# Attention feeding a mixture of experts: the order in which GpSimd issues value and weight loads

## The chip, the cores and the metric

The kernel runs on one NeuronCore of a Trainium2 chip. The metric is the device time of one execution in microseconds. The time before the change is 408.86 us, the median of 3 runs (408.62 to 410.64). The profile is of one execution of 408.99 us; its span, from the first instruction to the last, is 407.1 us.

## What is computed

Two layers, one after the other. The first is causal attention with two kinds of heads: three "retrieval" heads see every earlier key, five "streaming" heads see 4 sink keys and a window of 64. The second is a mixture of four experts in which every token goes through every expert.

```python
# attention: batch 4, heads 8, sequence 768, head size 64
scores = scale * np.matmul(q, k.transpose(0, 1, 3, 2))
mask = np.where(retr, full_causal_mask, stream_mask)   # stream: causal & (sink | window)
a = softmax(np.where(mask, scores, -1e9))
x = np.matmul(a, v)            # -> 3072 tokens x 512
# experts: N 3072, D 512, E 4, F 1024
p = domain_probs / (domain_probs.sum(-1, keepdims=True) + 1e-09)
for e in range(E):
    h = np.maximum(x @ w1[e], 0.0)
    out += p[:, e:e + 1] * (h @ w2[e])
```

## The kernel before

**Tiles and stages.** The 3072 tokens are cut into 8 groups of 384 (`CH`): 4 batches times 2 chunks. Group g first needs attention for its chunk (`attention`, L473), which leaves 384 token columns in `xT`, and then the experts (`moe_group`, L824). For each expert the first layer multiplies w1 with `xT` (L840, 32 matmuls of 384 columns), ScalarE applies the relu into `hs` (L853), the second layer multiplies `hs` with w2 (L861, 24 matmuls of 512 columns), and VectorE adds the scaled result into `acc` (L873, L877). Inputs are 32-bit in device memory, matrices are kept in 16-bit.

**What is interleaved.** Attention of group 0 runs alone at the start, on the head of the timeline. From then on attention of group g+1 is woven into the experts of group g: the loop at L897 draws from a generator of attention steps according to an estimate of work spent. All engines follow the order of the program (`manual_schedule`, L93); nothing is reordered by a planner.

**Weights.** All of w1 and w2 stay in on-chip memory for the whole kernel (`w1sb`, `w2sb`). `load_w1(e, 0, F)` (L296) issues two loads of 512 KB in 16-bit, one for each half of the partitions; `load_w2(e)` (L304) issues one of 1024 KB. Every weight is loaded once, during the experts of group 0, and the first use of expert e in group 0 waits for it.

**Keys, queries and values of batch 0.** Chunk 0: `k` and `q` come in 32-bit through the queues of SyncE and ScalarE (L355, L368). Chunk 1: `k` and `q` are one load each on GpSimd's queue, `load_triples` (L209, issue at L211), transposed on TensorE at L488. The values of both chunks are loaded by head with `load_v(b, c, heads)` (L264): a retrieval head (0, 2, 6) goes into `vR` (L268), a streaming head (1, 3, 4, 5, 7) into `vS` (L274), 48 KB each for batch 0. TensorE multiplies `vR` at L634 and `vS` at L698. In attention of chunk 0 the last value products are those of heads 6, 5 and 7, in this order, with filler matmuls (`warm_up`, L385) between them. In attention of chunk 1 the heads follow in the order 0, 2, 1, 3, 6, 5, 7, 4.

**GpSimd's queue.** All loads that change the number type go through GpSimd, which issues them in program order. Each load signals one of eight completion semaphores, taken in turn; before a load is issued GpSimd waits until the load eight places ahead, which used the same semaphore, has landed. Between the loads GpSimd fills padding and ones (`zero`, L327; `one_values`, L334; both through L325) and makes masks (L394 to L442). The order around the change is written out by hand at L445 to L463. After it come the fills of `kRr` and `kSr`, `mask_w`, and the loads for later groups (`load_k` L218, `load_q` L205, `load_v`), issued as far as the semaphores and buffers allow.

The loads of L445 to L463, in order: values of chunk 0 for heads 2, 1, 3, 4, 5, 6, 7 (head 0 was issued earlier, at L377); w1 of expert 0; fills; w2 of expert 0; k and q of chunk 1; w1 of expert 1; values of chunk 1 for heads 0 to 7; w2 of expert 1; w1 and w2 of experts 2 and 3.

Of the kernel before, what the change touches and what calls it, by code (L numbers as in the profile page):

```python
# [17 lines left out]
def kernel(  # L18
# [35 lines left out]
    B, H, S, D = q.shape  # L54
    E, DM, F = moe_w1.shape
# [93 lines left out]
    def half(u):  # L149
        return slice(u * D, (u + 1) * D)  # L150
# [5 lines left out]
    def own_v(h):  # L156
        return half(PLACE[h][1])
# [10 lines left out]
    def v_tiles(b, c, h):  # L168

        if RETR[h]:  # L170
            return vR[b % 2][:, 3 * c : 3 * c + 3, RH.index(h), :]
        if b:
            return windows(vSf, c)[:, :, SH.index(h), :]
        return vS[:, c, :, SH.index(h), :]
# [10 lines left out]
    def rows_of(x, b, h, c):  # L185
        return x[b, h, c * CH : (c + 1) * CH, :].rearrange("(j p) d -> p j d", p=P)

    def tiles_of(x, b, h, c):
        return x[b, h, c * CH : (c + 1) * CH, :].rearrange("(t r) d -> r t d", r=TK)

    def windows_of(x, b, h, c):

        assert b > 0
        first = ((b * H + h) * S + c * CH - WO) * D
        return bass.AP(x.tensor, x.offset + first, [[D, P], [WQ * D, WT], [1, D]])
# [68 lines left out]
    def load_v(b, c, heads):  # L264
        for h in heads:
            t = v_tiles(b, c, h)
            if RETR[h]:
                gp.dma_start(out=t[:, :, 0:D], in_=rows_of(v, b, h, c))  # L268
            elif b:
                gp.dma_start(  # L270
                    out=t[:, :, own_v(h)], in_=windows_of(v, b, h, c)
                )
            else:
                gp.dma_start(  # L274
                    out=t[R0:P, :, own_v(h)],
                    in_=tiles_of(v, b, h, c),
                )
# [18 lines left out]
    def load_w1(e, f0, f1):  # L296
        x = moe_w1[e].rearrange("(u c d) f -> u d c f", u=2, c=DMP)
        for u in range(2):
            gp.dma_start(  # L299
                out=w1sb[half(u), e * DMP : (e + 1) * DMP, f0:f1],  # L300
                in_=x[u, :, :, f0:f1],
            )

    def load_w2(e):  # L304
        gp.dma_start(
            out=w2sb[:, e * FTP : (e + 1) * FTP, :],
            in_=moe_w2[e].rearrange("(fo fi) d -> fi fo d", fi=P),
        )
# [6 lines left out]
    def fill(eng, ap, value):  # L315
        ap = ap.bitcast(FP32)
        if eng is nc.scalar:
            src = ones[0 : ap.shape[0], :]
            if len(ap.shape) == 3:
                src = src.rearrange("p (a b) -> p a b", a=1)  # L320
            elif len(ap.shape) == 4:
                src = src.rearrange("p (a b c) -> p a b c", a=1, b=1)
            eng.copy(out=ap, in_=src.to_broadcast(list(ap.shape)))
        else:
            eng.memset(ap, value)  # L325

    def zero(eng, t):  # L327
        fill(eng, t.rearrange("p a b x -> p (a b x)"), 0.0)
# [5 lines left out]
    def one_values(eng, c):  # L334

        one_values_r(eng, 0, c)
        x = vS[:, c, :, :, :].rearrange("p t s x -> p s t x")
        fill(eng, x[0:R0, :, :, :].rearrange("p s t x -> p (s t x)"), ONES)
        fill(eng, x[:, 0:2, :, D:P], ONES)
        fill(eng, x[:, 2:5, :, 0:D], ONES)  # L340
# [63 lines left out]
    def mask_s(x, n, keep, drop):  # L404

        gp.memset(x, keep)
        gp.affine_select(
            out=x, in_=x, compare_op=ALU.is_ge, fill=drop,
            base=R0, pattern=[[0, n], [1, TQ]], channel_multiplier=-1,
        )  # L410
        gp.affine_select(  # L411
            out=x, in_=x, compare_op=ALU.is_ge, fill=drop,
            base=NW - 1 - R0, pattern=[[0, n], [-1, TQ]], channel_multiplier=1,
        )
        gp.memset(x[0:R0, :, :], drop)
        gp.memset(x[0:NS, :, 0:TK], keep)
        gp.affine_select(
            out=x[0:NS, 0, 0:TK], in_=x[0:NS, 0, 0:TK], compare_op=ALU.is_ge,
            fill=drop, base=-NW, pattern=[[1, TK]], channel_multiplier=-1,
        )  # L420
# [23 lines left out]

    mask_c(bC, 0.0, -60000.0)  # L445
    mask_s(bS[:, 0:2, :], 2, 0.0, -60000.0)
    load_v(0, 0, [2, 1, 3, 4, 5, 6, 7])
    load_w1(0, 0, F)
    zero(gp, kR[0][:, 1, :, :, :])
    zero(gp, kS[:, 1, :, :, :].rearrange("p t s x -> p s t x"))  # L450
    one_values(gp, 1)
    load_w2(0)
    k16 = att.tile([P, H, 3, D], FP16, name="k16", bufs=1)
    load_triples(k, k16, 0, 1)
    qt16 = att.tile([P, H, 3, D], FP16, name="q16", bufs=2)
    load_triples(q, qt16, 0, 1)
    load_w1(1, 0, F)
    load_v(0, 1, range(H))
    load_w2(1)
    for e in range(2, E):  # L460
        load_w1(e, 0, F)
        load_w2(e)
    mSf = mS.rearrange("p t x -> p (t x)")  # L463
    bSf = bS.rearrange("p t x -> p (t x)")
    mWf = mW.rearrange("p t x -> p (t x)")
# [505 lines left out]
```

The softmax here doesn't subtract the row's maximum and nothing guards it: scores larger than these inputs give would overflow.

## Time and profile before

| engine | busy, us | share of the span |
|---|---|---|
| TensorE, matmuls | 393.4 | 97% |
| TensorE, weight loads (beside the matmuls) | 222.4 | 55% |
| ScalarE | 218.7 | 54% |
| VectorE | 156.0 | 38% |
| GpSimd | 142.8 | 35% |

The granted TensorE clock has a mean of 0.987 over the span. GpSimd's own queue moved 20.98 MB, counted as stored, in the whole span.

The groups of the page that bear on the change (operation, count, busy time, mean of one, idle time before it):

```profile
L840 PE MATMUL pA<-xT,w1sb 128*128 128x384 f16 x1024 | 188.3, 329 | 3.3 <-DMA w1sb<-in_moe_w_dram 3.1
L861 PE MATMUL pO<-w2sb,hs 128*128 128x512 f16 x768 | 182.4, 381 | 2.8 <-DMA w2sb<-in_moe_w_dram 2.8
L268 POOL DMA_DIRECT2D vR<-in_v_dram x24 | 19.3, 805 | 1.7 <-DMA w1sb<-in_moe_w_dram 1.6
```

And its list of loads (count, size of one, median time from issue to landing):

```profile
w1sb<-in_moe_w_dram POOLq DMA_DIRECT2D x8, 512.0 KB, 14.7
w2sb<-in_moe_w_dram POOLq DMA_DIRECT2D x4, 1024.0 KB, 14.8
```

Busy time of TensorE is the duration of its matmuls as the profile models them; a matmul at half the granted clock counts as busy for longer. The last column of a group is idle time of that engine just before such an instruction, with the releaser that ended most of it. A time from issue to landing includes the time that a load spends in the queue behind earlier ones.

### The profile page before, as it was taken

The page shows a single profiled execution, that of the slowest core. Times are in us where ns is not written, and L with a number is a line of the kernel's source. Part 1 is how long each engine was busy: PE and PEld are TensorE (multiplying, and loading weights), DVE is VectorE, ACT ScalarE, POOL GpSimd, SP SyncE. Part 2 cuts the span into 40 slices and gives each one's busy share as a digit, 9 for nine tenths or more (in the row PEclk, how much of TensorE's full clock was granted, in tenths as well). Part 3 has the DMA queues.
Part 4 walks back from the last instruction along what each step waited for, and adds up shares of the span by engine and source line. Part 5 has one row for each costly group of instructions (what it writes and reads, how often), then busy time and mean ns, then how long its engine had stood idle before and what let it go on. Part 6 is the DMA issues. An engine that isn't in the chain of part 4 may idle for free.

```text
span 407.1 us, 7111 instructions
## 1 busy us (share of the span) xinstructions
PE 393.4 (97%) x2821; PEld 222.4 (55%) x2821; DVE 156.0 (38%) x343; ACT 218.7 (54%) x468; POOL 142.8 (35%) x179
## 2 busy tenths in 40 slices
PE   7896799999999999999999999999999999999996
PEld 4753455555555555555555555555555555655552
DVE  7736065423443223434443223434443223432222
ACT  4751447734575456854464555854564555753331
POOL 8934922924954911950009600870000000000000
PEclk9997889999999999999999999999999999999999
DMA  9999999999998989990389929991391100010001
GB/s 169 143 182 143 183 205 185 99 159 172 120 182 142 145 91 158 98 162 10 53 148 111 148 39 161 78 182 21 47 148 52 31 11 0 11 77 2 0 2 78
DMA packets 165989, 42.23 MB, mean 104 GB/s; under 512 B 156380, under 2 KB 160836, under 8 KB 165956
## 3 DMA queue, kind: packets, MB, share of 16 engines
q0 software_dynamic: 102656, 20.98, 61.6%
q1 hardware_dynamic: 61700, 20.40, 25.6%
q10 hardware_dynamic: 1600, 0.39, 0.5%
q8 instruction: 22, 0.36, 0.4%
q14 instruction: 11, 0.09, 0.1%
HBM read 43.57 MB, written 6.29 MB: 122 GB/s over the span
## 4 chain that ended last, share of the span: by engine, by line
PE 86%; DMA 7%; POOL 5%; ACT 1%; issue 0%; DVE 0%; POOLq 0%
PE pO L861 40%; PE pA L840 37%; PE pA L586 5%; DMA w1sb<-in_moe_w_dram 4%; DMA w2sb<-in_moe_w_dram 3%; PE pV L634 2%; PE pV L698 2%; POOL vS L274 1%; ACT hs L853 1%; POOL vR L268 1%; POOL w1sb L299 0%; POOL vS L325 0%; POOL bS L411 0%; POOL kS L325 0%; ACT es L604 0%
## 5 line engine op out<-in xcount | busy, mean ns | idle before, releaser
L840 PE MATMUL pA<-xT,w1sb 128*128 128x384 f16 x1024 | 188.3, 329 | 3.3 <-DMA w1sb<-in_moe_w_dram 3.1
L861 PE MATMUL pO<-w2sb,hs 128*128 128x512 f16 x768 | 182.4, 381 | 2.8 <-DMA w2sb<-in_moe_w_dram 2.8
L853 ACT ACTIVATE hs<-pA 128x384 f16<-128x384 f32 x256 | 121.9, 492 | 100.5 <-PE pA L840 95.5
L840 PEld LDWEIGHTS <-w1sb 128*128 128x128 f16 x1024 | 97.0, 98 | 64.4 <-issue 5.8
L861 PEld LDWEIGHTS <-hs 128*128 128x128 f16 x768 | 71.6, 98 | 76.8 <-issue 3.5
L604 ACT ACTIVATE es<-pA 128x384 f16<-128x384 f32 (+2 forms) x122 | 61.2, 510 | 58.7 <-PE pA L586 56.0
L877 DVE SCALAR_TENSOR_TENSOR acc<-pO,p_sb,acc 128x512 f32<-128x512 f32 x72 | 54.1, 751 | 78.2 <-PE pO L861 77.5
L226 POOL DMA_DIRECT2D kSr<-in_k_dram x30 | 30.1, 1006 | 42.8 <-DMA kS<-kSr 23.6
L222 POOL DMA_DIRECT2D kRr<-in_k_dram x18 | 14.1, 785 | 72.9 <-DMA kR<-kRr 69.6
L721 DVE TENSOR_TENSOR xT<-pV,rc 64x384 f16<-64x384 f32 x37 | 20.5, 554 | 31.1 <-ACT rc L726 22.0
L608 DVE TENSOR_TENSOR es<-es,mC 128x256 f16<-128x256 f16 (+1 forms) x42 | 11.1, 264 | 54.4 <-ACT es L604 53.6
L270 POOL DMA_DIRECT2D vS<-in_v_dram x30 | 30.5, 1024 | 0.0
L873 DVE TENSOR_SCALAR acc<-pO,p_sb 128x512 f32<-128x512 f32 x24 | 18.0, 751 | 28.5 <-PE pO L861 28.2
L716 ACT ACTIVATE rc<-pV,eps 64x384 f32<-64x384 f32 x37 | 21.3, 575 | 12.2 <-PE pV L698 11.6
L586 PE MATMUL pA<-qT,kR 128*128 128x384 f16 (+2 forms) x120 | 25.9, 285 | 1.1 <-DVE kR L504 0.7
L726 ACT ACTIVATE rc<-rc 64x384 f32<-64x384 f32 x38 | 19.8, 521 | 1.2
L268 POOL DMA_DIRECT2D vR<-in_v_dram x24 | 19.3, 805 | 1.7 <-DMA w1sb<-in_moe_w_dram 1.6
L586 PEld LDWEIGHTS <-kR 128*128 128x128 f16 x120 | 11.8, 100 | 12.0 <-issue 1.8
L608 DVE TENSOR_TENSOR es<-es,mW 128x384 f16<-128x384 f16 x30 | 10.7, 358 | 17.1 <-ACT es L604 17.1
L634 PEld LDWEIGHTS <-es 128*128 128x128 f16 x252 | 13.4, 99 | 6.9 <-ACT es L604 0.6
L586 PEld LDWEIGHTS <-kS 128*128 128x128 f16 x255 | 13.3, 98 | 6.8
L698 PEld LDWEIGHTS <-vS 128*128 128x128 f16 x255 | 13.6, 98 | 6.2 <-issue 0.5
(91 smaller groups left out, 184.7 us busy)
## 6 DMA issues: line engine op xcount, KB each, us to landing
out_dram<-acc SPq DMA_DIRECT2D x24, 256.0 KB
w1sb<-in_moe_w_dram POOLq DMA_DIRECT2D x8, 512.0 KB, 14.7
w2sb<-in_moe_w_dram POOLq DMA_DIRECT2D x4, 1024.0 KB, 14.8
kSr<-in_k_dram POOLq DMA_DIRECT2D x30, 112.0 KB, 3.9
vS<-in_v_dram POOLq DMA_DIRECT2D x30, 112.0 KB, 5.0
q<-in_q_dram POOLq DMA_DIRECT2D x18, 128.0 KB, 4.4
vR<-in_v_dram POOLq DMA_DIRECT2D x24, 48.0 KB, 4.2
kRr<-in_k_dram POOLq DMA_DIRECT2D x18, 48.0 KB, 5.0
```

Source lines behind the costliest of these rows:

```text
L226: gp.dma_start(out=kSr[:, :, SH.index(h), own(h)], in_=windows_of(k, b, h, c),)
L268: gp.dma_start(out=t[:, :, 0:D], in_=rows_of(v, b, h, c))
L270: gp.dma_start(out=t[:, :, own_v(h)], in_=windows_of(v, b, h, c))
L586: nc.tensor.matmul(out=ps[:, o : o + nq], lhsT=key_tile(b, c, h, t), rhs=qTs[b, c][:, hp, q0 : q0 + nq], start=(n == 0 or not first), stop ...
L604: nc.scalar.activation(out=es[:, 0:cols], in_=ps[:, 0:cols], func=AF.Exp, scale=SC)
L608: nc.vector.tensor_tensor(out=es[:, o0:o1], in0=es[:, o0:o1], in1=m[:, mo : mo + o1 - o0], op=ALU.mult,)
L634: nc.tensor.matmul(out=ps[:, j, 0 : D + 1], lhsT=lhsT, rhs=vR[i][:, t, RH.index(h), 0 : D + 1], start=(n == 0), stop=(n == len(work) - 1), ...
L698: nc.tensor.matmul(out=ps[:, q0 : q0 + nq], lhsT=v_tile(b, c, h, t), rhs=es[:, o : o + nq], start=(n == 0), stop=(n == len(work) - 1), ski ...
L840: nc.tensor.matmul(out=pss[ft][:, 0:CH], lhsT=w1sb[:, e * DMP + ct, ft * P : (ft + 1) * P], rhs=xT[g][:, ct, :], start=(n == 0), stop=(n = ...
L853: nc.scalar.activation(out=hs[:, ft, :], in_=ps[:, 0:CH], func=AF.Relu)
L861: nc.tensor.matmul(out=ps_o, lhsT=hs[:, ft, j * P : (j + 1) * P], rhs=w2sb[:, e * FTP + ft, :], start=(ft == 0), stop=(ft == FTP - 1),)
L877: nc.vector.scalar_tensor_tensor(out=acc[nt], in0=ps_o, scalar=p_ap, in1=acc[nt], op0=ALU.mult, op1=ALU.add,)
```

## The change

The loads at L445 to L463 are put in another order. Weights of experts 0 to 2 now stand between the value loads: w1 of expert 0 comes after four of the value loads of chunk 0, w2 of expert 0 before the fills, w2 of expert 1 after two of the value loads of chunk 1, and w1 of expert 2 after five. The values of chunk 1 are issued in the order in which attention takes the heads. The purpose is that no run of eight outstanding loads holds up the issue of the next weights. No load, fill or matmul is added or taken away.

```diff
-    load_v(0, 0, [2, 1, 3, 4, 5, 6, 7])
+    load_v(0, 0, [2, 1, 3, 4])
     load_w1(0, 0, F)
+    load_v(0, 0, [5, 6, 7])
+    load_w2(0)
     zero(gp, kR[0][:, 1, :, :, :])
     zero(gp, kS[:, 1, :, :, :].rearrange("p t s x -> p s t x"))
     one_values(gp, 1)
-    load_w2(0)
     k16 = att.tile([P, H, 3, D], FP16, name="k16", bufs=1)
     load_triples(k, k16, 0, 1)
     qt16 = att.tile([P, H, 3, D], FP16, name="q16", bufs=2)
     load_triples(q, qt16, 0, 1)
     load_w1(1, 0, F)
-    load_v(0, 1, range(H))
+    load_v(0, 1, [0, 2])
     load_w2(1)
-    for e in range(2, E):
-        load_w1(e, 0, F)
-        load_w2(e)
+    load_v(0, 1, [1, 3, 6])
+    load_w1(2, 0, F)
+    load_v(0, 1, [5, 7, 4])
+    load_w2(2)
+    load_w1(3, 0, F)
+    load_w2(3)
```

More of the change, by code (lines that the diff above doesn't have):

```diff
@@ L457 @@
     load_w1(1, 0, F)
-    load_v(0, 1, range(H))
+    load_v(0, 1, [0, 2])
     load_w2(1)
-    for e in range(2, E):
-        load_w1(e, 0, F)
-        load_w2(e)
+    load_v(0, 1, [1, 3, 6])
[4 more added lines that the diff above has]
+    load_w2(3)
+    assert E == 4
     mSf = mS.rearrange("p t x -> p (t x)")
```

## The prediction

> **What bounds the kernel now.** I read the page first. TensorE is busy 393.4 of 407.1 us, so about 14 us can be had from its idle time; the row of granted clocks shows the other loss, tenths of 7, 8, 8 and 9 in slices 4 to 7 and 9 almost everywhere later. So whatever can be won lies in the first 60 us. The chain of work that ended last (start, length, what) says what sets the end there:
>
> ```profile
> 19.09 0.58 POOL w1sb L299
> 19.67 17.54 DMA w1sb<-in_moe_w_dram
> 37.50 0.70 POOL vS L274
> 38.20 10.60 DMA w2sb<-in_moe_w_dram
> 48.84 1.02 PE pO L861 x4
> ```
>
> Two weight loads of expert 1 carry the chain from 19 to 49 us; after that it is TensorE to the end. Here w1(e) and w2(e) are the two weight matrices of expert e, and v0 to v7 the value loads of one chunk by head. The timeline of TensorE shows what they cost (start, length, operation, idle time before it and what ended it):
>
> ```profile
> 17.57 0.22 PE L634 MATMUL pV<-vR,es 128*128 128x65 f16 x2
> 18.24 0.30 PE L634 MATMUL pV<-vR,es 128*128 128x65 f16 x4 [0.45 <-ACT es L604]
> ...
> 27.61 4.49 PE L861 MATMUL pO<-w2sb,hs 128*128 128x512 f16 x20 [0.52 <-DMA w2sb<-in_moe_w_dram]
> ...
> 37.35 1.44 PE L840 MATMUL pA<-xT,w1sb 128*128 128x384 f16 x4 [3.14 <-DMA w1sb<-in_moe_w_dram]
> 48.84 1.02 PE L861 MATMUL pO<-w2sb,hs 128*128 128x512 f16 x4 [2.24 <-DMA w2sb<-in_moe_w_dram]
> ```
>
> TensorE waits 0.52 us for w2(0), 3.14 us for w1(1) and 2.24 us for w2(1). Why w2(1) is late stands in GpSimd's timeline:
>
> ```profile
> 21.73 0.79 POOL L268 DMA_DIRECT2D vR<-in_v_dram  x1
> 27.85 0.71 POOL L274 DMA_DIRECT2D vS<-in_v_dram  x1 [5.33 <-DMA w2sb<-in_moe_w_dram]
> ...
> 34.74 0.75 POOL L268 DMA_DIRECT2D vR<-in_v_dram  x1 [1.57 <-DMA w1sb<-in_moe_w_dram]
> 37.50 0.71 POOL L274 DMA_DIRECT2D vS<-in_v_dram  x1 [2.00 <-DMA w1sb<-in_moe_w_dram]
> 38.20 0.91 POOL L305 DMA_DIRECT2D w2sb<-in_moe_w_dram  x1
> ```
>
> In GpSimd's instruction list each load reuses one of eight completion semaphores in turn, so it waits for the load eight places ahead. The value loads v3 to v7 of chunk 1 thereby wait one after another for w2(0), k, q and both halves of w1(1), and w2(1) behind them is issued at 38.20, when w1(1) has already landed. Short windows show what this does to the DMA and to the clock (last three numbers: granted clock, DMA share, GB/s):
>
> ```profile
> 15.50:16.00 0.50, 0.50 (x6) 0.45 (x5) 0.47 (x3) 0.48 (x2) 0.44 (x2) 1.00 0.35 66
> 36.50:37.00 0.50, 0.00 (x0) 0.00 (x0) 0.50 (x1) 0.00 (x0) 0.00 (x0) 0.50 3.08 125
> 38.00:38.50 0.50, 0.50 (x3) 0.24 (x2) 0.00 (x0) 0.00 (x0) 0.50 (x2) 0.50 0.43 27
> 39.50:40.00 0.50, 0.50 (x4) 0.18 (x2) 0.12 (x1) 0.35 (x1) 0.50 (x2) 0.50 0.44 24
> 50.00:50.50 0.50, 0.50 (x5) 0.16 (x2) 0.00 (x0) 0.00 (x0) 0.50 (x1) 0.51 1.13 213
> ```
>
> The queue runs at 190 GB/s from 23 to 36 us and 203 from 44 to 60, but is nearly empty from 38 to 40.5 (19 to 45 GB/s in four of five half microseconds) and around 15.5. After each long wait the clock is halved: windows of 0.5 us put the first dip at 36.4 to 43.2 us and the second at 50.0 to 53.4 us.
>
> [...]the windows 32.95:36.36 and 46.6:50.0 were busy 1.26 and 1.16 us of 3.4 and a dip followed; 36.36:39.77, busy 2.42, stayed halved; 5.65:9.06, busy 2.60, halved nothing. [...]all of GpSimd's loads up to 50 us land in order of issue. [...]v7 of chunk 1, 48 KB into a nearly empty queue, took 2.4 us from issue. And w2(1), issued after it, took 10.6 us where w2(2), queued in time, landed 5.1 us after its predecessor: a weight load issued late loses up to 5.5 us that a queued one hides.
>
> **The change, part by part.** [...]Nothing of TensorE's, ScalarE's, VectorE's or SyncE's order changes.
>
> Landing times before (issue plus time to landing of each load): v4 to v7 of chunk 0 14.1 to 15.0; w1(0) 20.8; w2(0) 27.5; k 29.6; q 32.2; w1(1) 37.2; v0 to v7 of chunk 1 37.6 to 39.9; w2(1) 48.8; w1(2) 53.7; w2(2) 58.8; w1(3) 65.4; w2(3) 70.3.
>
> (a) w1(0) is issued ahead of three value loads of 0.7 us, so at 9.5 instead of 11.6 us, and w2(0) ahead of 3.6 us of fills, at about 12.9 instead of 16.4. The k, q and w1(1) loads keep their places in the list (17.3 to 20.3 us); the semaphores they now wait for belong to v3, v4 and the halves of w1(0), landed by then within half a microsecond. The 0.9 us hole around 15.5 closes, because w1(0) already stands in the queue. v4 lands near 14.0; w1(0) at about 14.0 + 5.0 = 19.0; v5, v6, v7 at 0.3 us each behind it (three took 0.9 before), 19.3, 19.6, 19.9; w2(0) 19.9 + 6.7 = 26.6; and k, q and w1(1) all 0.9 us earlier than before, w1(1) at 36.3. Ends: 35.5 (value loads behind w1(1) no longer disturb its tail) to 37.2 (no hole really closed).
>
> (b) The price: v6, wanted by TensorE at 17.57, lands at 19.6. Behind the waiting matmul stand the rest of attention 0 and the first layer of expert 0. The six matmuls end near 19.8 instead of 18.37: a delay of d = 1.4 us (0.5 to 2.5), up to 2.9 if the clock is halved from 19.3 to 22.7. But from the first expert matmul (21.46) to the wait for w1(1) there are 34.21 - 21.46 = 12.75 us, of which 0.52 (w2(0)) and 0.16 (q) were waits that the earlier landings remove. TensorE is ready for w1(1) at 33.5 + d = 34.9 and starts it at 36.4, when it is there. All delays up to 2.8 us lie in that wait and cost nothing.
>
> (c) w2(1) moves ahead of six value loads. It now waits for v7 of chunk 0 (19.9) and is issued near 22 instead of 38.2. In the queue it stands behind w1(1), v0 and v2 (0.7 us): 36.3 + 0.7 + 5.1 to 6.7 (the fastest and slowest w2 in a full queue) = 42.1 to 43.7; I take the middle, 42.9, instead of 48.8. TensorE wants it after 46.6 - 37.35 = 9.25 us of work, of which 5.84 us ran at half clock, so 2.9 us are clock. At full clock it is 6.3 us: 36.4 + 6.3 = 42.7. Second layer of expert 1: 42.9, against 48.84.
>
> (d) The wait before w1(1) shrinks from 3.14 to about 1.5 us, that before w2(1) from 2.24 to 0.2. Windows with 2 us or more of work are then likely, and no dip. The second dip cost 3.4 us at half speed, 1.7 us.
>
> (e) v1, v3, v6 land after w2(1) (about 44), v5, v7, v4 after w1(2) (about 48.5); heads 1 and 5 are first multiplied at 60.15 and after 75 us, less 8: free. w1(2), about 48, is wanted at 58.0 - 7.6 = 50.4; w2(2), issued when w2(1) has landed, about 53.5, at 64.6 - 7.6 = 57; w1(3) and w2(3) have more room. GpSimd's later fills (43.3 to 49.1) move some 3 us back; the loads behind them waited for w2(2), w1(3), w2(3) until 70 us anyway, and these land earlier. Free.
>
> Sum: 48.84 - 42.9 = 5.9 earlier, plus 1.7 of the second dip: 7.6 us, and TensorE alone sets the rest. 408.86 - 7.6 = 401.3 us.
>
> **The rivals.** Clock stays low once: the remaining wait, or the one for v6, still halves a window that matters. No window with 1.3 to 2.4 us busy was seen at full clock[...]. One window costs 1.7, two 2.9 (as in the first dip), less the 0.2 that hides in the wait for w2(1): 402.8 to 404.0 us. Bytes decide: w1(1) lands at 37.2 as before, since the bytes ahead of it are the same, and its wait and dip stay; only 2.24 + 1.7 = 3.9 us go: 405.0. For it, the queue's share was 1.0 or more from 16 to 36 us; against it, the hole at 15.5. Hidden anyway: w2(1) lands no earlier because the queue, not the issue, was slow after 37 us: 408.5. Against it, 24 GB/s with nothing else queued. Slower: v6 lands at 21.7, and TensorE stays at half clock from 19.3 to about 39[...]. d is 3.5 plus half of the 17.3 us from 21.7 to 39, 12.2: w1(1) starts at 45.7, w2(1)'s layer at 52.0, and 3.2 later less 1.7 is +1.5; one more half-clock window makes it +3.2: 412. Against it, the first layer of expert 0 is 5.64 us without a gap[...].
>
> **How the numbers follow.** Forecast 0.53, clock once 0.24, bytes decide 0.15, hidden anyway 0.05, slower 0.03. The low end is w1(1) at 35.5, w2(1)'s layer at 41.9, 6.9 + 1.7 = 8.6: 400.2. The high end takes in "bytes decide": 405.2. Faster 0.92, within 0.5% 0.05, slower 0.03.
>
> **What would show it.** In the changed profile: w2(1) issued near 22 us and landed near 43; w1(1) landed 36.3; a new wait of about 2 us for vR before L634 near 17.6; no wait for w2sb above 0.5 us; a clock of 1.00 from 37 to 54; no weight wait after 50 us. The prediction is wrong if w1(1) lands no earlier, if GpSimd's queue holds w2(1) back for another reason, or if the clock falls during the wait for v6 and isn't back by 36 us.

## The result, and the profile after

The changed kernel takes 403.49 us, the median of 4 runs (402.10 to 404.42), against 409.50 us (408.62 to 410.64) for the kernel before: a ratio of 0.985, with a 95% interval of 0.981 to 0.989. A second set of runs gave 402.45 us against 410.17, a ratio of 0.982 (0.979 to 0.984). The forecast was 401.3 us with a range of 400.2 to 405.2. The span of the profiled execution falls from 407.1 to 402.0 us. In the changed kernel the lines after the diff stand 7 lower: L840 is now L847, L861 is L868, L634 is L641.

The timeline of TensorE after the change, at the places shown of before (start, length, operation, idle time before it and its releaser):

```profile
17.63 1.01 PE L387 MATMUL pV<-warm 128*128 128x256 f16 x4 [3.56 <-DVE x_pair L661]
...
22.33 0.64 PE L641 MATMUL pV<-vR,es 128*128 128x65 f16 x6
...
25.89 5.63 PE L847 MATMUL pA<-xT,w1sb 128*128 128x384 f16 x32
...
39.99 1.46 PE L847 MATMUL pA<-xT,w1sb 128*128 128x384 f16 x8 [1.09 <-DVE qT L504]
...
45.35 1.03 PE L868 MATMUL pO<-w2sb,hs 128*128 128x512 f16 x4
```

All waits for weights are gone. The second layer of expert 1 starts at 45.35 instead of 48.84. But a new wait of 3.56 us stands in attention 0, for VectorE, and the first expert matmul is 4.4 us late (25.89 instead of 21.46). The chain of work that ended last names it (start, length, what):

```profile
12.19 0.56 DVE kS L527
12.75 0.09 DVE kS L535
12.84 0.03 issue
12.87 3.91 DVE vS L282
16.78 0.03 issue
16.81 0.17 DVE rs L654
```

L282 is `sink_row`: VectorE copies the sink values of one head, 4 rows of 256 elements, from 32 to 16 bits. Before, the five such copies took 0.27 to 0.43 us each. The fifth, for head 7, took 0.28 us, from 12.71; now it takes 3.91. GpSimd's timeline of the same kernel:

```profile
12.86 0.94 POOL L305 DMA_DIRECT2D w2sb<-in_moe_w_dram  x1
13.74 0.65 POOL L325 MEMSET kR<- 128x576 f32 x1
14.26 1.24 POOL L325 MEMSET kS<- 128x1280 f32 x1
15.36 0.18 POOL L325 MEMSET vR<- 128x9 f32 x1
15.40 1.99 POOL L325 MEMSET vS<- 32x1280 f32 x3
...
20.38 1.50 POOL L268 DMA_DIRECT2D vR<-in_v_dram  x2
21.87 0.93 POOL L305 DMA_DIRECT2D w2sb<-in_moe_w_dram  x1
25.59 0.69 POOL L274 DMA_DIRECT2D vS<-in_v_dram  x1 [2.79 <-DMA w2sb<-in_moe_w_dram]
```

The issue of w2 of expert 1 is at 21.87 instead of 38.20, as the change intends. And the copy of 12.87 to 16.78 lies on top of a run of GpSimd instructions from 12.86: the issue of w2(0), then the fills. The short windows (last three numbers: granted clock, DMA share, GB/s):

```profile
15.50:16.00 0.50, 0.00 (x0) 0.00 (x0) 0.50 (x1) 0.00 (x0) 0.50 (x2) 1.00 1.06 197
17.50:18.00 0.50, 0.37 (x2) 0.26 (x2) 0.50 (x3) 0.00 (x0) 0.50 (x1) 0.50 1.32 175
20.00:20.50 0.50, 0.50 (x4) 0.38 (x3) 0.22 (x1) 0.42 (x2) 0.50 (x2) 0.50 1.21 203
38.00:38.50 0.50, 0.48 (x3) 0.09 (x1) 0.47 (x2) 0.00 (x0) 0.00 (x0) 1.00 1.26 211
50.00:50.50 0.50, 0.50 (x14) 0.41 (x14) 0.43 (x1) 0.20 (x1) 0.50 (x1) 1.00 1.19 199
```

The hole in the queue at 15.5 us is closed (197 GB/s, 66 before), and so is the one at 38 (211, 27 before). The two clock dips of before are gone; a single one, 17.3 to 20.7 us, follows the new wait.

The account of the 5.1 us of span, from the two timelines: the first expert matmul is 4.4 us later. From there to the second layer of expert 1 it is 45.35 - 25.89 = 19.5 us instead of 48.84 - 21.46 = 27.4, so 7.9 less: 5.0 of waits (0.52 + 0.16 + 3.14 + 2.24 before, 1.09 after) and 2.9 of clock (in the first dip of before eight first-layer matmuls took 2.76 us, at 39.01, and behind it 1.46, at 44.10). Behind it the second dip is gone, 1.7 us. In all 4.4 - 7.9 - 1.7 = -5.2.

### The profile page after: what moved, and what is told of

It reads as the page before. It is cut to its first block, busy times and chain, and to the rows that moved or that the text cites. A ratio compares the mean times of both kernels' runs of the same rounds, so it can differ in the third digit from the quotient of the medians.

```text
span 402.0 us, 7112 instructions
## 1 busy us (share of the span) xinstructions
PE 390.6 (97%) x2821; PEld 222.2 (55%) x2821; DVE 159.3 (40%) x343; ACT 218.6 (54%) x468; POOL 142.1 (35%) x179
## 3 DMA queue, kind: packets, MB, share of 16 engines
q1 hardware_dynamic: 61700, 20.40, 26.3%
## 4 chain that ended last, share of the span: by engine, by line
PE 94%; DVE 3%; ACT 2%; issue 0%
PE pO L868 41%; PE pA L847 41%; PE pA L593 5%; PE pV L705 2%; PE pV L641 2%; PE pO L387 1%; DVE vS L282 1%; ACT hs L860 1%; PE pA L495 0%; ACT es L611 0%; PE pA L492 0%; DVE qT L504 0%; ACT rc L723 0%; DVE xT L728 0%; DVE kS L527 0%
## 5 line engine op out<-in xcount | busy, mean ns | idle before, releaser
L847 PE MATMUL pA<-xT,w1sb 128*128 128x384 f16 x1024 | 185.8, 326 | 1.2 <-DVE qT L504 1.1
L868 PE MATMUL pO<-w2sb,hs 128*128 128x512 f16 x768 | 181.1, 379 | 0.0
L847 PEld LDWEIGHTS <-w1sb 128*128 128x128 f16 x1024 | 96.2, 98 | 61.0 <-issue 1.8
L868 PEld LDWEIGHTS <-hs 128*128 128x128 f16 x768 | 71.4, 98 | 73.0 <-ACT hs L860 0.7
L611 ACT ACTIVATE es<-pA 128x384 f16<-128x384 f32 (+2 forms) x122 | 61.3, 510 | 54.6 <-PE pA L593 52.6
L728 DVE TENSOR_TENSOR xT<-pV,rc 64x384 f16<-64x384 f32 x37 | 20.5, 553 | 31.7 <-ACT rc L733 22.1
L880 DVE TENSOR_SCALAR acc<-pO,p_sb 128x512 f32<-128x512 f32 x24 | 18.0, 751 | 27.6 <-PE pO L868 27.4
L733 ACT ACTIVATE rc<-rc 64x384 f32<-64x384 f32 x38 | 19.8, 521 | 1.2
L641 PEld LDWEIGHTS <-es 128*128 128x128 f16 x252 | 13.2, 97 | 6.5 <-ACT es L611 0.2
```

Source lines behind the costliest of these rows:

```text
L611: nc.scalar.activation(out=es[:, 0:cols], in_=ps[:, 0:cols], func=AF.Exp, scale=SC)
L641: nc.tensor.matmul(out=ps[:, j, 0 : D + 1], lhsT=lhsT, rhs=vR[i][:, t, RH.index(h), 0 : D + 1], start=(n == 0), stop=(n == len(work) - 1), ...
L847: nc.tensor.matmul(out=pss[ft][:, 0:CH], lhsT=w1sb[:, e * DMP + ct, ft * P : (ft + 1) * P], rhs=xT[g][:, ct, :], start=(n == 0), stop=(n = ...
L868: nc.tensor.matmul(out=ps_o, lhsT=hs[:, ft, j * P : (j + 1) * P], rhs=w2sb[:, e * FTP + ft, :], start=(ft == 0), stop=(ft == FTP - 1),)
```

## The experiments

Two questions were left by the result. What holds the copy, and is it part of the change's price? And which part of the order brings the gain? The table has the landing times of the profiled execution of each kernel, us from the span's start; "start" is the first expert matmul, "layer 2" the first matmul with w2 of expert 1. Each ratio is to runs of the kernel before taken in the same set, whose medians were 409.5 to 410.4 us.

| kernel | w1(0) | w2(0) | w1(1) | w2(1) issued | w2(1) | start | layer 2 | median us | ratio to before (95%) |
|---|---|---|---|---|---|---|---|---|---|
| before | 20.8 | 27.5 | 37.2 | 38.2 | 48.8 | 21.5 | 48.8 | | |
| after | 19.6 | 25.3 | 34.9 | 21.9 | 41.5 | 25.9 | 45.4 | 403.49 | 0.985 (0.981 to 0.989) |
| after_again | 19.6 | 25.6 | 35.1 | 22.0 | 40.7 | 23.0 | 42.6 | 402.45 | 0.982 (0.979 to 0.984) |
| first_part | 19.8 | 25.7 | 35.4 | 36.3 | 47.4 | 23.2 | 47.5 | 407.38 | 0.995 (0.993 to 0.997) |
| second_part | 20.6 | 27.7 | 39.3 | 21.8 | 46.2 | 21.0 | 47.0 | 404.44 | 0.989 (0.987 to 0.991) |
| w2_ahead | 20.6 | 26.1 | 35.9 | 36.9 | 47.4 | 21.7 | 47.4 | 408.26 | 0.995 (0.993 to 0.996) |
| sink_early | 19.8 | 25.6 | 34.7 | 22.1 | 41.1 | 24.7 | 44.1 | 402.48 | 0.983 (0.981 to 0.984) |
| fills_late | 19.4 | 25.4 | 34.4 | 25.3 | 40.6 | 22.5 | 42.0 | 403.05 | 0.984 (0.982 to 0.987) |
| copy_hit | 19.5 | 25.3 | 34.6 | 21.9 | 40.4 | 23.7 | 43.2 | 402.81 | 0.984 (0.980 to 0.987) |
| copy_free | 19.4 | 25.3 | 35.2 | 25.3 | 41.4 | 22.7 | 42.2 | 402.75 | 0.982 (0.979 to 0.985) |
| sink_v6 | 20.5 | 26.3 | 35.9 | 22.3 | 42.1 | 22.5 | 42.3 | 403.45 | 0.983 (0.980 to 0.985) |
| w2_2_early | 19.6 | 25.2 | 35.7 | 21.8 | 42.0 | 21.6 | 43.7 | 403.85 | 0.986 (0.983 to 0.988) |

**sink_early: the copy out of GpSimd's way.**

```diff
             sink_row(5)
+            sink_row(7)
 ...
             yield from transposes(2)
-            sink_row(7)
```

> The changed kernel with one edit: VectorE's copy of the sink values of head 7 (the one that took 3.91 us at 12.87 us) is moved ahead, right behind those of heads 4 and 5, to about 10 us, where GpSimd issues loads and fills nothing. [...]the copy takes 0.3 to 0.5 us, TensorE's wait of 3.56 us for x_pair is gone, and only the wait for the values of head 6, which land at 19.9, is left, about 2 us near 17.8. First expert matmul near 23.1 instead of 25.9, w1 of expert 1 (landing 34.9) reached with no wait or a short one, total 403.5 - 2.7 = 400.8 us, ratio to before near 0.979. Rival 'DMA' (something in the load traffic of 13 to 16.6 us held VectorE or TensorE there, and the copy only stood in its way): another VectorE instruction near 13 us takes as long, total stays near 403.5.

The longest of the five copies takes 0.54 us, and the wait for x_pair is gone. What TensorE then waits for in this kernel (us in total, times, longest):

```profile
PE pV L641 <- DMA vR<-in_v_dram: 2.4, 1, 2.4
PE pO L387 <- DVE warm L372: 1.3, 1, 1.3
PE pA L847 <- DVE qT L504: 1.1, 1, 1.1
```

The values of head 6 are the next limit, as the prediction had it: they land at 20.2 us, and TensorE waits 2.4 us for them. The total came out at 402.48 instead of 400.8 us, because the clock is again at half behind that wait, from 20.2 to 23.6 us, which costs 1.7 us, and the first expert matmul is at 24.7 instead of 23.1. The rival is out: no VectorE instruction from 12.2 to 16.5 us takes more than 0.56 us. But in the total, no price of the stall shows: the changed kernel's second set has 402.45 us.

**fills_late: the same place of the copy, no fills.**

```diff
     load_w2(0)
-    zero(gp, kR[0][:, 1, :, :, :])
-    zero(gp, kS[:, 1, :, :, :].rearrange("p t s x -> p s t x"))
-    one_values(gp, 1)
 ...
     load_w1(1, 0, F)
+    zero(gp, kR[0][:, 1, :, :, :])
+    zero(gp, kS[:, 1, :, :, :].rearrange("p t s x -> p s t x"))
+    one_values(gp, 1)
```

> The changed kernel with one edit: GpSimd's fills for chunk 1 (3.6 us, 13.74 to 17.4) are moved behind the issue of w1 of expert 1, and everything else stays. The copy of head 7's sink values stays where it was, at 12.87. [...]the copy ends by 13.9 us, when GpSimd is through with the issue of w2 of expert 0; first expert matmul near 23.1, total near 400.8. [...]Rival 'DMA' (the copy waits for the landing of w1 of expert 0, first half, at 16.6 us): it still ends at 16.6 and the total stays near 403.5.

The copy takes 0.28 us at 12.87, and the first expert matmul is at 22.5. The landing of w1(0)'s first half, at 16.9 us here, has nothing to do with it, so the DMA rival falls. But the copy starts within 0.01 us of the issue of w2(0), at 12.88, and in the changed kernel it stood 0.01 us on the other side of it. So this run cannot tell whether the issue or the fills would have held it; the next two separate them. The total, 403.05, is not the 400.8 that was expected.

**copy_hit and copy_free: the copy moved into the fills, and into loads without fills.** Both move the copy behind the scores of head 4, where it starts at 14.22 and 13.83 us; copy_free also has the fills behind w1(1), as above.

```diff
             yield from transposes(2)
-            sink_row(7)
 ...
             yield from scores(4)
+            sink_row(7)
             yield from transposes(3)
```

> The changed kernel with VectorE's copy of head 7's sink values moved back by some 1.5 us, to about 14.3, so that it falls with certainty into GpSimd's fills (13.7 to 17.4 us) and not into the issue of a load. [...]the copy takes from 14.3 to the pause inside the fills at 16.65 us, some 2.3 us, and no GpSimd instruction is lengthened. Rival 'the issue of w2 of expert 0 held it': the copy takes 0.3 us here. The total says little: a stall of 2.3 us for the scores of head 6 lies in front of the wait for the values of head 6 (19.9), so near 402.5.

> The same place of the copy, but GpSimd's fills behind the issue of w1 of expert 1, so that around 14.3 us GpSimd issues the k load and then the q load (13.8 to 15.6) and pauses. Fills theory: the copy takes 0.3 to 0.5 us. Rival 'issues hold it too': until 14.65 or 15.6, so up to 1.3 us. Rival 'DMA landing': still to 16.6. Total 402 to 403.

VectorE's and GpSimd's timelines of copy_hit:

```profile
14.22 2.61 DVE L282 CAST vS<-v_s 4x256 f16<-4x256 f32 x1
```

```profile
12.94 0.90 POOL L305 DMA_DIRECT2D w2sb<-in_moe_w_dram  x1
13.83 0.61 POOL L325 MEMSET kR<- 128x576 f32 x1
14.34 1.20 POOL L325 MEMSET kS<- 128x1280 f32 x1
15.45 0.14 POOL L325 MEMSET vR<- 128x9 f32 x1
15.49 1.95 POOL L325 MEMSET vS<- 32x1280 f32 x3
17.39 0.88 POOL L211 DMA_DIRECT2D k<-in_k_dram  x1
```

VectorE's timeline of copy_free, where GpSimd issues the k load from 13.77 to 14.69:

```profile
13.83 0.27 DVE L282 CAST vS<-v_s 4x256 f16<-4x256 f32 x1
```

In the fills the copy takes 2.61 us, without them 0.27. It ends at 16.83, in the changed kernel at 16.78: both times 1.3 to 1.4 us into the last group of three fills. There lies the only gap in the run of fills: the second vS fill starts 0.06 and 0.05 us after the first has ended (16.63 and 16.69), every other one before its predecessor has. No fill is lengthened: they take as long in sink_early, where no copy is near (0.64, 1.23, 0.17 and 1.95 us). So the copy that started within the fills was held over four of them in a row and ended at their first gap, 2.61 us after its start. By what mechanism is not shown. In the changed kernel the first fill starts only at 13.74, so what held the copy from 12.87 until then is not shown by these two. The issue of a k load, from 13.77 to 14.69, did not hold one (0.27 us in copy_free).

The totals, 402.81 and 402.75 us, do not differ beyond their spread, as expected: in copy_hit the stall lies in front of the wait for the values of head 6 and takes its place (2.64 us for kR, none for vR).

**after_again: is the stall there every time?**

> The changed kernel itself once more, for a closer interval and to see whether the stuck copy of head 7's sink values (3.91 us in the first profile) comes in every execution. Theory 'race of 0.3 us': the copy starts between 12.6 and 13.0 us and GpSimd's issue of w2 of expert 0 at 12.9, so some executions have the stall and some don't: times spread from 401.5 to 404.5, median near 403.3, ratio to before near 0.984. If the stall comes always, the spread is within 1 us around 403.9.

VectorE's timeline of that execution of the same kernel:

```profile
12.62 0.17 DVE L535 CAST kS<-pA 64x16 f16<-64x16 f32 x1
12.82 1.09 DVE L282 CAST vS<-v_s 4x256 f16<-4x256 f32 x1
13.94 0.16 DVE L654 TENSOR_SCALAR rs<-pV 128x3 f32<-128x3 f32 x1
```

Here the copy starts 0.05 us earlier and ends at 13.91, 0.16 us into the first fill. TensorE waits 0.74 us for x_pair and 1.5 for the values of head 6, and the first expert matmul is at 23.0. In first_part, with the same order up to there, the copy took 0.49 us. So the stall differs from execution to execution. But the start of the copy against that of w2(0)'s issue does not decide it alone. In w2_ahead, below, where the fills follow that issue as in the changed kernel, the copy starts later than in the first profile and is not held:

```profile
12.86 0.94 POOL L305 DMA_DIRECT2D w2sb<-in_moe_w_dram  x1
12.97 0.31 DVE L282 CAST vS<-v_s 4x256 f16<-4x256 f32 x1
```

What makes the copy miss its turn is therefore open. The four times of this set lay between 402.25 and 402.78 us, without the spread that was expected; the first set had it (402.10 to 404.42), but so had fills_late (401.12 to 405.13), whose profiled copy is short, so a spread of times does not count the stalls. Only two executions of the changed kernel were profiled, and how often the stall comes is open too.

**first_part: only the loads up to w1 of expert 1 reordered.**

```diff
-    load_v(0, 1, [0, 2])
-    load_w2(1)
-    load_v(0, 1, [1, 3, 6])
-    load_w1(2, 0, F)
-    load_v(0, 1, [5, 7, 4])
-    load_w2(2)
-    load_w1(3, 0, F)
-    load_w2(3)
+    load_v(0, 1, range(H))
+    load_w2(1)
+    for e in range(2, E):
+        load_w1(e, 0, F)
+        load_w2(e)
```

> Only the first part of the change: w1 and w2 of expert 0 moved ahead; the loads after w1 of expert 1 in the old order. [...]the copy is stuck as in the changed kernel (3.9 us), first expert matmul near 25.9, w1(1) lands near 35; w2(1) is issued only when w1(1) has landed, near 36, and lands near 46.5, so that TensorE, which wants it at 45.2, waits about 1.3 us: total near 404.8. If instead the first part alone is the gain (bytes decide, and the early issue of w2(1) is worth nothing): 403.5.

The ratio is 0.995, some 2.3 us less than before; 407.38 us against 404.8 expected. TensorE's timeline:

```profile
35.48 0.81 PE L843 MATMUL pA<-xT,w1sb 128*128 128x384 f16 x4 [0.36 <-DMA w1sb<-in_moe_w_dram]
...
47.49 1.87 PE L864 MATMUL pO<-w2sb,hs 128*128 128x512 f16 x4 [4.58 <-DMA w2sb<-in_moe_w_dram]
```

The first layer of expert 1 starts 1.9 us earlier than before, the second only 1.4 (47.5 instead of 48.8), for w2(1) is issued at 36.3 and lands 11.1 us later. The expected wait was 1.3 us; it is 4.6, because the copy was not stuck in this execution and TensorE stood at w2(1) earlier, at 42.9 instead of 45.2, and because w2(1) landed 0.9 later than expected. In that wait the clock also falls to half, from 45.8 to 52.6. The early issue of w2(1) is needed for the rest of the gain.

**second_part: only the loads after w1 of expert 1 reordered** (the same lines the other way, in the kernel before).

> Only the second part of the change: the loads after w1 of expert 1 in the new order, those before it in the old one. Attention 0 as before (copy 0.3 us, first expert matmul at 21.5), w1(1) lands at 37.2 and the wait of 3.1 us and the clock dip behind it stay; w2(1) is issued near 22 and lands near 43, so its wait of 2.2 us and the second dip (1.7 us) go: 3.9 us less than before, near 405.2. If w1(1)'s earlier landing in the changed kernel comes from this part (fewer small loads behind it), w1(1) lands near 35 and the total is near 402.5.

The ratio is 0.989, about 4.6 us less than before, where 3.9 was expected. In the profiled execution, which was 2.4 us above the median of its kernel, w1(1) lands at 39.3, so its earlier landing does not come from this part. TensorE's timeline:

```profile
39.41 1.44 PE L844 MATMUL pA<-xT,w1sb 128*128 128x384 f16 x4 [3.46 <-DMA w1sb<-in_moe_w_dram]
...
47.01 1.03 PE L865 MATMUL pO<-w2sb,hs 128*128 128x512 f16 x4
```

The wait for w1(1) stays and that for w2(1) is gone, as expected. The larger of the two parts is this one. It moves other loads too, but what TensorE shows of it up to the second layer of expert 1 is that the wait for w2(1), now issued 16 us earlier, is gone.

**w2_ahead: why w1(1) lands earlier.**

```diff
     load_w1(0, 0, F)
+    load_w2(0)
     zero(gp, kR[0][:, 1, :, :, :])
 ...
     one_values(gp, 1)
-    load_w2(0)
```

> The kernel before with one edit: w2 of expert 0 is issued ahead of the fills (at 12.9 instead of 16.4 us), everything else in the old order. It asks why w1 of expert 1 lands 2.3 us earlier in the changed kernel. If only the hole in the queue at 15.5 us counts (0.9 us) and the rest was chance: w1(0) lands 20.8, w2(0) 27.5, w1(1) 37.2 as before, total within 0.5 us of before. If the distance between issue and turn counts (w2(0) took 6.7 us of the queue when issued 4.4 us ahead of its turn, 5.1 us when issued 7 us ahead): w2(0) lands near 25.9, w1(1) near 35.6, and TensorE's wait for it falls from 3.1 to 1.5 us; w2(1) is still issued only after that landing, so its wait grows; total 1 us less than before at most.

w2(0) lands at 26.1 and w1(1) at 35.9, 1.3 us earlier than before, and the wait for w1(1) falls to 2.5 us. w2(1), still issued only after that landing, comes 1.4 us earlier too, and TensorE, which is there sooner, waits 3.3 us for it. The total is 2.1 us less than before, where 1 at most was expected. In seven profiled executions that issue w2(0) at 12.9 us (after, after_again, copy_hit, copy_free, w2_ahead, sink_v6, w2_2_early) it lands 5.0 to 5.5 us after the load in front of it; in the two that issue it at 16.4, before and second_part, 6.7 and 7.1 us. So the early issue gives 1.2 us or more of queue time beside the closed hole. By what mechanism is open.

**sink_v6: towards a faster version.** The copy early as in sink_early, and the values of head 6 ahead of w1(0).

```diff
-    load_v(0, 0, [2, 1, 3, 4])
+    load_v(0, 0, [2, 1, 3, 4, 6])
     load_w1(0, 0, F)
-    load_v(0, 0, [5, 6, 7])
+    load_v(0, 0, [5, 7])
```

> The version that the runs so far point to: the changed kernel with head 7's sink copy early (no clash with GpSimd) and the values of head 6 loaded ahead of w1 of expert 0 ([2, 1, 3, 4, 6], then w1, then [5, 7]). Theory: attention 0 no longer waits for v6 (landing near 15 instead of 19.9), so no idle of 2.4 us and no clock dip behind it; first expert matmul near 21.7; then w1(1), landing near 34.8, sets the pace with a wait of 1 us; total 402.5 - 1.7 = 400.8 us. If v5 and v7, still behind w1(0), come too late, a wait for vS near 19 takes the place of that for vR: 401.5 to 402.5.

The start is at 22.5 and no clock dip is left, but the total, 403.45 us against 400.8 expected, is no better than after: TensorE waits 1.1 us for vS of head 5, which now is the late one, and 2.6 us for w2 of expert 2. Three short windows of this kernel, from 52.0 us, show why w2 of expert 2 is late:

```profile
52.00:52.50 0.50, 0.50 (x8) 0.39 (x7) 0.46 (x2) 0.39 (x1) 0.43 (x2) 1.00 4.26 116
52.50:53.00 0.50, 0.50 (x5) 0.29 (x3) 0.00 (x0) 0.47 (x2) 0.50 (x4) 1.00 0.96 32
53.00:53.50 0.50, 0.50 (x6) 0.30 (x4) 0.00 (x0) 0.47 (x2) 0.43 (x2) 1.00 0.19 9
```

The queue runs dry around 53 us although w2(2) was issued at 43.3, and w2(2) lands at 59.0.

**w2_2_early: is that a late issue again?**

```diff
     load_w1(2, 0, F)
-    load_v(0, 1, [5, 7, 4])
     load_w2(2)
+    load_v(0, 1, [5, 7, 4])
```

> The version before (sink copy early, v6 ahead of w1 of expert 0) with w2 of expert 2 moved ahead of the last three value loads of chunk 1, so that it no longer waits behind the load which waits for the landing of w2 of expert 1: issued near 37 instead of 43.3 us. Theory 'late issue again': w2(2) lands near 54 instead of 59, TensorE's wait of 2.6 us for it goes, total 403.45 - 2 = 401.4 us. Rival 'the gap in the queue at 52 to 54 us comes from something else than the issue' (the DMA transpose of x_one issued just before, at 46.7 us): the gap stays, w2(2) or a later weight waits for it, total near 403.

w2(2) is issued at 36.6 and lands at 55.5, and TensorE's wait for it is gone. But a hole remains, 26 GB/s at 54.0, so it does not come from the late issue alone. It lies 5 to 6 us behind the issue of the DMA transpose of x_one, at 48.2; in sink_v6 the transpose is issued at 46.7 and the hole begins at 52.5, in the changed kernel at 49.8 and 55.5, in after_again at 47.0 and 52.0, in copy_hit at 47.6 and 53.0. That speaks for the transpose. But elsewhere the rate falls less at that distance: to 118 GB/s in fills_late, to 133 in first_part and to 169 in the kernel before. No run changed the transpose, so it is not shown. The total is 403.85 us. Neither version beats the changed kernel. In w2_2_early TensorE waits 2.26 us before the first layer of expert 1, until 35.81, and the clock is halved from 36.0 to 39.5. That wait ends as w1(1) lands (35.7), but VectorE's copy into qT ends within 0.1 us of it, so which of the two sets the pace is not shown.

## Why the prediction was right, and where it was not

**The bound and the gain.** Right. The two holes in the queue and the late issue of w2(1) were what the change removed. From the first expert matmul to the second layer of expert 1 the prediction had 42.9 - 22.9 = 20.0 us; measured were 19.5, in after_again 19.6. Both dips of before went, worth 2.9 and 1.7 us.

**(a) The landings.** The closed hole: right. w1(0) was forecast at 19.0 and landed at 19.6, v6 at 19.6 and 19.9, w2(0) at 26.6 and 25.3, w1(1) at 36.3 and 34.9. The mis-sized term is w2(0) in the queue, taken over as 6.7 us; issued early it needs 5.0.

**(b) The price.** In the first profile this step failed by its size. It had d = 1.4 us, up to 2.9 with the clock; the first profile has 4.4: a wait of 3.56 us in place of some smaller ones, 2.9 us net, and 1.5 us of clock (TensorE worked from 17.63 to 20.69 at half). The cause was not the wait for v6, which the stall swallowed, but the copy that took 3.91 us beside GpSimd's instructions, the fills from 13.74 on. The step failed in the sentence that nothing of VectorE's order changes. That is true and beside the point: what counts is also how VectorE's work lies in time against GpSimd's (the same copy took 2.61 us in copy_hit and 0.27 in copy_free). In the profile of before the copy is at 12.71 us and the fills begin at 12.85, so the neighbourhood could have been read there. That the change brought the stall about is not shown: before, the copy escaped by a little, and with w2(0) issued ahead of the fills it escaped too in w2_ahead (0.31 us). In after_again the copy is held for 1.1 us only, and d is 1.5, as forecast.

**That delays up to 2.8 us cost nothing.** Right in kind. In after_again the start is 1.5 us late and TensorE still waits 0.34 us for w1(1), so nothing of the delay was paid. In the first profile w1(1) landed at 34.9 and TensorE came for it at 37.66: of the 4.4 us of delay, 2.8 were paid. As w1(1) landed 1.4 us before its forecast, the room was 1.4 us smaller than the 2.8 of the prediction.

**(c) and (d).** Right: w2(1) issued at 21.9 and landed at 41.5 (forecast 42.9), no wait for it, clock 1.00 from 36 to 54 us. Instead of none, one dip is left, 17.3 to 20.7. So of the rivals "clock stays low once" came true in part, in front of the experts and not within them; "bytes decide" fell with the landing of w1(1), "hidden anyway" with that of w2(1), and "slower" with the clock, which was back after 3.4 us, in which TensorE was busy 3.06.

**(e).** Right that no weight is waited for after 50 us. w2(2), forecast at 53.5, landed at 55.1 and was wanted at 59.5; in after_again it landed at 56.8 and was used at 56.9, so there the room was gone.

**The sum.** Forecast 7.6 us less than 408.86, measured 6.0 less than 409.50 in the first set and 7.7 less than 410.17 in the second. In the profiled execution of the first set the span fell by 5.1 us, and the 2.5 us missing are the later second layer of expert 1, 45.35 instead of 42.9. About half of it is the term d: the first layer of expert 1 starts at 37.66 instead of 36.4. The other half is a wait in that layer which the prediction did not have, 1.09 us for VectorE's copy into qT; after_again shows it too (0.89 us). Of the other executions of that set no profile is on record.

## What to carry to other kernels

A load that is held up in a queue's issue order can pay twice, as w2(1) did here: it missed its turn in the DMA queue, and it started into a nearly empty one (10.6 us from issue for 1 MB, against about 5 behind the load in front when it is queued in time); so look for the loads whose issue waits for the landing of one that has just become slow, and put small, not urgent loads behind them. When instructions of GpSimd are moved, look at what VectorE copies at that time: here a run of fills without a gap held a copy of 0.3 us for 2.6 us. Fills that stood later left the copy free, though the kernel was no faster for it (403.05 and 402.75 us). And price a wait of TensorE with the clock that follows it: here a wait of 2.2 us (w2(1), before) cost 1.7 us more, while one of 2.6 us in sink_v6 was followed by no dip.

## What the runs showed of the hardware that was not expected

- A copy of 4 by 256 elements on VectorE took 2.61 us when it started inside GpSimd's fills and 0.27 us without them. Started within 0.11 us of an issue that fills follow, it took 0.31, 1.09 and 3.91 us in three executions. The two longest ended at the only gap in the run of fills.
- The clock was at half for 3.4 us (17.28 to 20.69 in the changed kernel, 20.22 to 23.64 in sink_early, 38.8 to 42.2 in second_part, 36.0 to 39.5 in w2_2_early, 50.0 to 53.4 before) or for 6.8 us (36.4 to 43.2 before, 45.8 to 52.6 in first_part). In the 3.41 us in front of a dip TensorE was busy 0.20 us (changed kernel), 1.00 (sink_early), 1.26 and 1.16 (before). Two dips of 3.4 us ended with 3.06 (changed kernel) and 2.80 us (second_part) busy in them; the first dip of before went on after 3.41 us with 2.42 busy.
- w2 of expert 0, 1 MB, took 5.0 to 5.5 us of the queue in seven executions that issued it 7 us or more ahead of its turn, and 6.7 and 7.1 us in the two that issued it about 4 us ahead.
- Some 5 to 6 us after the DMA transpose of x_one was issued, the DMA rate fell to 9 to 60 GB/s in five profiled executions, to 118 and 133 in two others and to 169 in the kernel before; whether the transpose is the cause is open.
